# A pause in the due table of the weight conversions, in a fused attention and expert kernel

## The chip, the cores and the metric

One NeuronCore of a Trainium2 chip runs the whole kernel. The metric is the time of one execution on the device in microseconds (us). Five engines work beside one another, each on a queue of its own: PE (TensorE; its weight loads are shown as PEld), DVE (VectorE), ACT (ScalarE), POOL (GpSimd) and SP (SyncE), which here only issues DMAs.

## The reference

Causal attention in blocks of 64 over 8 batches of 8 heads (sequence 576, head size 64), then a feed-forward layer (512 to 2048 to 512) on its output:

```python
scores = scale * np.matmul(q, k.transpose(0, 1, 3, 2))
scores = np.where(mask, scores, -1000000000.0)
scores = scores - np.max(scores, axis=-1, keepdims=True)
attn = np.exp(scores)
attn = attn / (np.sum(attn, axis=-1, keepdims=True) + 1e-09)
attn_out = np.matmul(attn, v)
x = attn_out.transpose(0, 2, 1, 3).reshape(B * S, H * D)
h = x @ w_in
g = h * (1.0 / (1.0 + np.exp(-1.702 * h)))
return g @ w_out
```

The inputs q, k and v are float32. The two weight matrices are float64, and the kernel makes float32 of their bits itself, from the two 32-bit words of each weight.

## The kernel before, in words

**Attention by turns.** Two heads make a pair, and there are 32 pairs. Turn n (n from 0) computes the scores of pair n and the sums of values of pair n-1. A turn is a list of slots, written out by hand (ORDER, START for turn 4, HANDOVER for turn 8). In a slot stands a dash or one item:

- digits such as `1+0`, `2/3`, `4`: scores of these chunks of queries (`score`: matmuls into a PSUM bank, line 351 adds the mask and finds the maximum on DVE, line 358 is the exponential on ACT, lines 368 and 371 turn the sums into factors on DVE, line 376 scales on POOL, into the tile `turned` in the first 8 turns)
- `B`, `C`, `a`: flips of the weights of attention on PE (`flip`, line 102), moved out of PSUM by ACT (lines 411 and 424)
- `V`: the sums of values of pair n-1 (`av`, ACT lines 450 and 451 bring them to the tile `xr`), and the value loads of a later pair (`load_v`, lines 287 and 290)
- `L`: `prep` of pair n+1: two transposes on DVE (line 297, q first and then k), and then, into the buffer that they have just read, the eight loads of q and k of pair n+2 (`load`, line 279)

A slot's position is twice the turn plus its part of the turn. The list of turn 4, and the one of turns 5 to 7, are

```python
START = "1+0 - B 2/3 L C - V - 4 - a - - -"
"1+0 - B - 2 - C - 3 L V - a - 4 -",
```

so that L of turn 4 stands at position 8.67, its V at 9.07, its `4` at 9.33, and L of turn 5 at 11.25.

**The expert layer by tiles.** The 4608 tokens are 12 tiles of 384. For each of 16 slices of 128 columns of the hidden layer (`fc`), 12 matmuls sum into `hp`, ACT (line 562) and DVE (563) make `g` of it, ACT (571) its high part `gh` and POOL (82) the low part `gl`, and 9 matmuls sum `g` times the output weights into `acc`, one slice later. Matmuls take float32r, so that each operand is a high and a low part, and a product is three matmuls. Tile 0 starts after the sums of values of pair 3 (V of turn 4); from there on its matmuls stand between the items of the turns, as many after each slot as TILES_BY says. All matmuls are recorded at lines 99 and 102, helpers that keep PE in the order of the program.

**The weights by pieces.** 32 pieces of 128 by 512 weights, in groups of 8: four pieces of w_in, then four of w_out. Slices 4g to 4g+3 need group g: `hp` all four w_in pieces (8g to 8g+3, one after another), `acc` of slice fc the piece 8g + 4 + fc % 4. Each piece is two steps:

- `merge` (step 2j), on DVE: lines 223, 229 and 234 make float32 of the two words. Before it stands `begin` (line 219, ACT), which scales the high word into the PSUM bank `w3`, the only one for this
- `split_weights` (step 2j+1): the high part on ACT (line 243, tile `wih` or `woh`), the low part on POOL (line 82, `wil` or `wol`). With it go the load of piece j+2 on SP (line 202) and the `begin` of piece j+1

```python
if odd:
    split_weights(j)
    if j + 1 < len(pieces):
        load_weights(j + 3)
        begin(j + 1)
```

**What sets the order.** After each slot the loop at the end calls `convert` with the number of pieces due by then: WEIGHTS_BY, read off by linear interpolation at the slot's position less 0.5, and doubled and rounded down for steps (lines 631 and 632). So the table says where in the program a step, its loads and its begin are emitted. A slice of tile 0 also calls `convert` for what it needs (line 543), if it isn't emitted yet. The framework then gives each engine one fixed queue when the program is built. Matmuls keep the program's order; of the other instructions it takes the one earliest in the program among those that are ready by its own estimates of times. On the chip each engine works through its queue in that order.

Of the kernel before, what the change touches and what calls it, by code (L numbers as in the profile page):

```python
# [32 lines left out]
HANDOVER = "B C - 3+0/2+1 - - V - - - 4 - - L - -"  # L33


WEIGHTS_BY = ((0, 0), (8, 13), (14.5, 32))
TILES_BY = ((8.4, 0), (17, 1), (33.7, 4), (65.7, -2))


# [1 line left out]
def attention_moe_kernel(  # L41
# [204 lines left out]
    def convert(upto):  # L246

        while conv["step"] < int(2 * upto):
            j, odd = divmod(conv["step"], 2)
# [5 lines that stand above are left out]
            else:  # L255
                if j == 0:
                    begin(0)
                merge(j)
            conv["step"] += 1
# [322 lines left out]
    def quota(pos):  # L582
        xs, ys = zip(*TILES_BY)
        return -1.0 if pos < xs[0] else np.interp(pos, xs, [ends[y if y >= 0 else y - 1] for y in ys])
# [39 lines left out]
    for n in range(NPAIR + 1):  # L624
        items = step(n)
        for sl, fn in enumerate(items):
# [4 lines left out]
            pos = 2 * (n + (sl + 1) / len(items))  # L631
            convert(min(len(pieces), np.interp(pos - 0.5, *zip(*WEIGHTS_BY))))
            lim = quota(pos)
# [31 lines left out]
```

## Time and profile before

| | us |
|---|---|
| median of 3 runs | 1123.53 |
| lowest and highest | 1121.69 and 1123.55 |
| the profiled execution | 1120.49 |
| its span, first to last instruction | 1118.6 |
| busy: ACT | 498.6 (45%) |
| busy: POOL | 406.7 (36%) |

The rows that follow below are from this profiled execution. A row of a group has the line, the engine, what is written and read, shapes, the count, and the shortest, middle and longest duration in ns. A row of the timeline has the start in us, the duration in us, the engine ("SPq" is SP's issuing of DMAs), the line, the operation and the tiles; in brackets stand the idle time before it and what ended it. For a DMA the duration is that of its issue. Times count from the start of the span.

### The profile page before, as it was taken

The page shows a single profiled execution, that of the slowest core. Times are in us where ns is not written, and L with a number is a line of the kernel's source. Part 1 is how long each engine was busy: PE and PEld are TensorE (multiplying, and loading weights), DVE is VectorE, ACT ScalarE, POOL GpSimd, SP SyncE. Part 2 cuts the span into 40 slices and gives each one's busy share as a digit, 9 for nine tenths or more (in the row PEclk, how much of TensorE's full clock was granted, in tenths as well). Part 3 has the DMA queues.
Part 4 walks back from the last instruction along what each step waited for, and adds up shares of the span by engine and source line. Part 5 has one row for each costly group of instructions (what it writes and reads, how often), then busy time and mean ns, then how long its engine had stood idle before and what let it go on. Part 6 is the DMA issues. An engine that isn't in the chain of part 4 may idle for free. (4 is left out here: it accounts for less than half of the span.)

```text
span 1118.6 us, 19977 instructions
## 1 busy us (share of the span) xinstructions
PE 1076.4 (96%) x6960; PEld 908.7 (81%) x6960; DVE 583.0 (52%) x1856; ACT 498.6 (45%) x1321; POOL 406.7 (36%) x509
## 2 busy tenths in 40 slices
PE   5969998999999999999999999999999999999998
PEld 3757776788888888888888888888888888899997
DVE  6776885545545555654555655645545654211210
ACT  5866776434534433534443543444434444322322
POOL 4665664333333332333333333333333233122222
PEclk9979999999999999999999999999999999999999
DMA  8734532332444432343443333344342332200000
GB/s 171 205 89 153 150 73 62 84 79 57 105 86 86 103 80 64 64 98 78 98 101 74 75 93 65 70 108 85 81 107 63 71 85 58 54 29 1 29 1 29
DMA packets 219365, 91.25 MB, mean 82 GB/s; under 512 B 197760, under 2 KB 197760, under 8 KB 219264
## 3 DMA queue, kind: packets, MB, share of 16 engines
q1 hardware_dynamic: 214528, 89.38, 34.0%
q10 hardware_dynamic: 4736, 0.59, 0.3%
q8 instruction: 55, 0.90, 0.3%
q14 instruction: 46, 0.38, 0.1%
HBM read 45.09 MB, written 9.44 MB: 49 GB/s over the span
## 5 line engine op out<-in xcount | busy, mean ns | idle before, releaser
L82 POOL TENSOR_TENSOR gl<-g,gh 128x384 fp32r<-128x384 f32 x192 | 194.7, 1014 | 551.5 <-ACT gh L571 449.1
L99 PE MATMUL hp<-xh,wih 128*128 128x384 f32 x768 | 264.7, 345 | 7.9 <-DVE g L563 6.9
L563 DVE SCALAR_TENSOR_TENSOR g<-g,hp 128x384 f32<-128x384 f32 x192 | 105.9, 552 | 319.1 <-ACT g L562 317.8
L99 PE MATMUL hp<-xh,wil 128*128 128x384 f32 x768 | 258.4, 336 | 0.1
L562 ACT ACTIVATE g<-hp 128x384 f32<-128x384 f32 x192 | 94.1, 490 | 359.8 <-PE hp L99 354.8
L99 PE MATMUL hp<-xl,wih 128*128 128x384 f32 x768 | 253.9, 338 | 0.4 <-DVE xl L82 0.4
L99 PE MATMUL acc<-woh,gh 128*128 128x512 f32 x576 | 233.9, 406 | 0.0
L99 PE MATMUL acc<-wol,gh 128*128 128x512 f32 x576 | 226.9, 394 | 0.0
L99 PEld LDWEIGHTS hp<-xh,wih 128*128 128x128 f32 x768 | 144.2, 188 | 34.1 <-DVE g L563 23.1
L99 PE MATMUL acc<-woh,gl 128*128 128x512 f32 x576 | 167.9, 393 | 0.3 <-POOL gl L82 0.3
L571 ACT CAST gh<-g 128x384 fp32r<-128x384 f32 x192 | 98.4, 513 | 156.5 <-DVE g L563 156.4
L99 PEld LDWEIGHTS hp<-xh,wil 128*128 128x128 f32 x768 | 144.3, 188 | 6.5 <-POOL wil L82 0.7
L358 ACT ACTIVATE e<-e,mx 64x64 f32<-64x64 f32 (+4 forms) x240 | 132.3, 552 | 37.6 <-DVE mx L351 37.6
L376 POOL TENSOR_TENSOR e<-e,sm 64x64 f32<-64x64 f32 (+1 forms) x192 | 113.6, 612 | 95.0 <-DVE sm L371 46.5
L99 PEld LDWEIGHTS hp<-xl,wih 128*128 128x128 f32 x768 | 143.6, 188 | 1.3 <-DVE xl L82 1.3
L99 PE MATMUL bank<-qk 64*128 64x320 f32 (+4 forms) x768 | 122.5, 428 | 14.5 <-DVE qk L297 11.1
L99 PEld LDWEIGHTS acc<-woh,gh 128*128 128x128 f32 x576 | 107.9, 187 | 34.2 <-issue 10.5
L99 PEld LDWEIGHTS acc<-woh,gl 128*128 128x128 f32 x576 | 107.8, 188 | 25.9 <-POOL gl L82 1.2
L99 PEld LDWEIGHTS acc<-wol,gh 128*128 128x128 f32 x576 | 108.3, 188 | 16.7 <-POOL wol L82 0.3
L351 DVE CUSTOM_DVE_ANT_0 e<-bank,mask 64x64 f32<-64x64 f32 (+4 forms) x240 | 89.7, 417 | 56.9 <-PE bank L99 52.8
L385 DVE STREAM_TRANSPOSE turned<-e 128x384 f32<-128x384 f32 (+1 forms) x192 | 92.3, 499 | 48.8 <-POOL e L376 48.3
L99 PEld LDWEIGHTS bank<-qk 64*128 64x128 f32 x768 | 69.6, 193 | 54.2 <-issue 25.4
(50 smaller groups left out, 956.0 us busy)
## 6 DMA issues: line engine op xcount, KB each, us to landing
turned<-turned SPq DMA_DIRECT2D x192, 80.0 KB, 2.1
turned<-turned SPq DMA_DIRECT2D x96, 112.0 KB, 2.2
raw<-in_q_dram SPq DMA_DIRECT2D x128, 72.0 KB, 2.4
out_dram<-osb SPq DMA_DIRECT2D x36, 256.0 KB, 2.2
raw<-in_k_dram SPq DMA_DIRECT2D x120, 72.0 KB, 2.6
turned<-turned SPq DMA_DIRECT2D x96, 88.0 KB, 2.1
words<-in_moe_w_in_dram SPq DMA_DIRECT2D x16, 512.0 KB, 6.3
vp<-in_v_dram SPq DMA_DIRECT2D x60, 128.0 KB, 2.4
```

The lines of the kernel that those rows point to most:

```text
L82: eng.tensor_tensor(out=out, in0=in0, in1=in1, op=ALU.subtract)
L99: return tc.keep_in_program_order(nc.tensor.matmul(**kw))
L351: nc.vector.tensor_tensor_reduce(out=e[0:m, hd, lo:hi], in0=s, in1=mk, op0=ALU.add, op1=ALU.min, scale=-0.125, scalar=3e38 if lo == 0 else ...
L358: nc.scalar.activation(out=e[0:m, hd], in_=e[0:m, hd], func=AF.Exp, scale=-1.0, bias=mx[0:m, i, hd : hd + 1], accum_out=sm[0:m, i, hd : hd ...
L376: nc.gpsimd.tensor_tensor(out=x, in0=x, in1=sc.to_broadcast([m, width(i)]), op=ALU.mult)
L385: nc.vector.transpose(out=tw[:, :, SLOT[i] : SLOT[i] + i, hd].rearrange("p b j c -> p j b c"), in_=e[:, hd, 0 : i * P],)
L562: nc.scalar.activation(out=g, in_=hp[:, 0:tt], func=AF.Tanh, scale=1.702)
L563: nc.vector.scalar_tensor_tensor(out=g, in0=g, scalar=1.0, in1=hp[:, 0:tt], op0=ALU.add, op1=ALU.mult)
L571: nc.scalar.copy(out=gh, in_=g)
```

## The change

One constant is changed, the table of due pieces:

```diff
-WEIGHTS_BY = ((0, 0), (8, 13), (14.5, 32))
+WEIGHTS_BY = ((0, 0), (7.5, 12), (8.8, 12.5), (14.5, 32))
```

Between the points 7.5 and 8.8 (slot positions 8.0 to 9.3, turn 4 up to its `4`) the table grows by half a piece only. Before it the slope is 1.6 pieces for a unit of position and was 1.625; after it 3.42, and was 2.92. In steps (half pieces) due after a slot:

| position | slot | steps before | steps after |
|---|---|---|---|
| 5.43 | dash before V, turn 2 | 16 | 15 |
| 6.71 | dash before L, turn 3 | 20 | 19 |
| 8.00 | end of turn 3 | 24 | 24 |
| 8.53 | `2/3`, turn 4 | 26 | 24 |
| 9.20 | dash after V, turn 4 | 30 | 24 |
| 9.47 | dash after `4`, turn 4 | 31 | 26 |
| 11.00 | dash before `3`, turn 5 | 40 | 36 |
| 11.25 | L, turn 5 | 42 | 38 |
| 11.50 | dash after V, turn 5 | 43 | 40 |
| 13.00 | dash before `3`, turn 6 | 52 | 50 |
| 13.25 | L, turn 6 | 53 | 52 |
| 14.13 | `1+0`, turn 7 | 58 | 58 |
| 15.00 | dash after C, turn 7 | 64 | 64 |

Step 2j+1 counts as done at 2j+2; with it the load of piece j+2 is emitted. No instruction is added or taken away.

## The prediction

> **What bounds the kernel now.** I read the page's busy times first, then PE by stretches of 10 us over the time in which weights are converted, then what PE waited for in it.
>
> ```profile
> PE 1076.4 (96%) x6960; PEld 908.7 (81%) x6960; DVE 583.0 (52%) x1856; ACT 498.6 (45%) x1321; POOL 406.7 (36%) x509
> 60.00:70.00 10.00, 6.08 (x19) 3.57 (x18) 7.82 (x26) 7.67 (x24) 5.05 (x7) 0.52 0.87 215
> 70.00:80.00 10.00, 9.08 (x83) 7.57 (x82) 8.07 (x16) 6.24 (x18) 6.54 (x8) 0.80 0.07 29
> 120.00:130.00 10.00, 8.23 (x49) 6.35 (x50) 9.52 (x32) 8.02 (x23) 6.45 (x6) 1.00 0.55 166
> 130.00:140.00 10.00, 10.00 (x54) 7.72 (x53) 7.43 (x19) 6.82 (x18) 7.05 (x11) 1.00 0.44 123
> 180.00:190.00 10.00, 6.91 (x43) 5.69 (x43) 3.16 (x10) 5.58 (x16) 5.09 (x5) 1.00 0.06 13
> 900.00:1000.00 100.00, 99.75 (x639) 87.33 (x638) 36.38 (x110) 35.69 (x87) 28.21 (x33) 1.00 0.22 57
> ```
>
> In a stretch's row the columns after the length are busy PE, PEld, DVE, ACT and POOL, the granted clock, the DMA share and GB/s. PE is the bound over the whole span, and late in it (900 to 1000) it hardly pauses, so what PE loses before 200 us is carried to the end, and what it wins there too. The question is only what the change does to PE's pauses up to 200 us. From 82 us on, when the first expert slice is through, these are:
>
> ```profile
> PE bank L102 <- ACT turned L411: 3.5, 3, 1.6
> PE bank L102 <- POOL turned L376: 3.1, 2, 2.0
> PE bank L99 <- DVE mx L351: 2.5, 4, 1.5
> PE hp L99 <- DVE g L563: 1.8, 1, 1.8
> ```
>
> (Total, number, longest.) That is 10.9 us between 82 and 205 us, none of it put down to a converted weight. The weights come just in time, though, as the rows of the third part show.
>
> **What the change moves.** It removes and adds no instruction. Up to the start of turn 4 the due table falls by at most one step in a slot; from there to the end of turn 6 it is 1 to 6 steps (half pieces) lower. Two things follow.
>
> First the conversions' own order. A piece is a chain over three engines with one PSUM buffer:
>
> ```profile
> L219 ACT ACTIVATE wm<-words x28: 612/633/662, 13.2 to 159.3; 128x512 f32<-128x512 f32 x28
> L223 DVE TENSOR_SCALAR wm<-wm x32: 658/699/700, 18.1 to 180.3; 128x512 uint32<-128x512 uint32 x32
> L243 ACT CAST woh<-wm x16: 617/620/641, 57.9 to 183.9; 128x512 fp32r<-128x512 f32 x16
> L82 POOL TENSOR_TENSOR wol<-wm,woh x16: 1262/1286/1302, 60.3 to 185.9; 128x512 fp32r<-128x512 f32 x16
> ```
>
> The 28 first halves (line 219) are pieces 0 to 27 in order, the last at 159.28, so any of them can be counted. The table asks for all 64 steps by the middle of turn 7, yet the last low part starts at 185.9, among the scalings of that turn's last score, nearly half a turn later: the chain runs several pieces behind its due table, at the pace of its own links. A due time that moves while the chain is behind it changes nothing by itself. I cost this part at nothing; its cover is that backlog.
>
> Second, the loads. The split of piece j also issues the load of piece j+2, on SP, and SP's issues stand in the trace in the order in which the program emits them. Behind the loads of q and k for a later pair (line 279) an issue is stuck until the transposes of line 297 free the buffer:
>
> ```profile
> 88.59 0.77 DVE L297 STREAM_TRANSPOSE qk<-raw 128x576 f32<-128x576 f32 x1
> 89.39 1.95 SPq L279 DMA_DIRECT2D raw<-in_q_dram  x4
> 91.39 2.12 SPq L279 DMA_DIRECT2D raw<-in_k_dram  x4
> 93.55 0.50 SPq L202 DMA_DIRECT2D words<-in_moe_w_out_dram  x1
> 98.18 0.64 ACT L219 ACTIVATE wm<-words 128x512 f32<-128x512 f32 x1
> 101.17 0.63 ACT L243 CAST woh<-wm 128x512 fp32r<-128x512 f32 x1
> 110.49 0.77 DVE L297 STREAM_TRANSPOSE qk<-raw 128x576 f32<-128x576 f32 x1
> 111.64 0.63 ACT L219 ACTIVATE wm<-words 128x512 f32<-128x512 f32 x1
> ```
>
> The load at 93.55 is piece 15's, the first behind the eight q/k loads of pair 6. Piece 14 begins at 98.18 and is split at 101.17; then the chain stands still until 111.64, where piece 15 begins, 0.38 us after the transpose that uses those q/k loads has ended. Its load had been issued 18 us before. So the fixed order of ACT, made when the program is built, counts a load behind the q/k loads as landing only with them. I take this from the place of the row; it is what the forecast hangs on.
>
> By the due tables four sets of loads change sides. Piece 11 goes behind the q/k loads of pair 5 (split 9 is due after the slot L of turn 3, not before it), piece 14 behind those of pair 6 (split 12 at 9.47, past L of turn 4 at 8.67), pieces 20 and 21 behind those of pair 7 (splits 18 and 19 at 11.25 and 11.50, L at 11.25), piece 27 behind those of pair 8. (Piece 9 passes the four value loads of pair 3; the backlog hides that.) The issues themselves are SP's and nothing waits for SP's time.
>
> **The cost.**
>
> ```profile
> 84.94 0.65 ACT L219 ACTIVATE wm<-words 128x512 f32<-128x512 f32 x1
> 90.99 0.62 ACT L219 ACTIVATE wm<-words 128x512 f32<-128x512 f32 x1
> 131.69 1.27 POOL L82 TENSOR_TENSOR wil<-wm,wih 128x512 fp32r<-128x512 f32 x1
> 133.95 0.34 PE L99 MATMUL hp<-xh,wil 128*128 128x384 f32 x1
> 135.06 1.28 POOL L82 TENSOR_TENSOR wol<-wm,woh 128x512 fp32r<-128x512 f32 x1 [2.10 <-ACT woh L243]
> 135.27 0.65 ACT L219 ACTIVATE wm<-words 128x512 f32<-128x512 f32 x1
> 139.43 0.63 ACT L219 ACTIVATE wm<-words 128x512 f32<-128x512 f32 x1
> 154.40 0.64 ACT L219 ACTIVATE wm<-words 128x512 f32<-128x512 f32 x1
> 159.28 0.64 ACT L219 ACTIVATE wm<-words 128x512 f32<-128x512 f32 x1
> 161.29 1.28 POOL L82 TENSOR_TENSOR wil<-wm,wih 128x512 fp32r<-128x512 f32 x1
> 162.62 0.44 PE L99 MATMUL hp<-xh,wil 128*128 128x384 f32 x1
> 163.11 1.28 POOL L82 TENSOR_TENSOR wil<-wm,wih 128x512 fp32r<-128x512 f32 x1 [0.54 <-ACT wih L243]
> 164.44 0.44 PE L99 MATMUL hp<-xh,wil 128*128 128x384 f32 x1
> ```
>
> Step 1. Piece 11 begins where piece 12 did (90.99 for 84.94), pieces 12 and 13 in the places of 13 and 14, and then the pause comes one piece earlier: piece 14 begins at 111.64. Pieces 14 to 19 stand in the places of 15 to 20. Before, piece 19's low part ends at 131.69 + 1.27 = 132.96 and PE reads it at 133.95, a slack of 0.99. In piece 20's place it ends at 135.06 + 1.28 = 136.34: PE waits 136.34 - 133.95 = 2.4 us in hp of slice 8. Queued behind on PE are the rest of that slice and the scores and flips of turn 6, and for these DVE and ACT wait.
>
> Step 2. Piece 20 now has a load behind the q/k loads of pair 7. It begins between 135.27 (piece 21's place, if the load holds nothing) and 139.43 (the place of piece 22, the first behind these loads before). Neither row says which, since piece 22's predecessor ended just then: I take the middle, 137.35.
>
> Step 3. From piece 15 to 27 the pace is (159.28 - 111.64) / 12 = 3.97 us. Six pieces on, piece 26 begins at 161.2 (159.1 to 163.3) in place of 154.40: 6.8 us late (4.7 to 8.9). It has no slack: its low part ends at 161.29 + 1.28 = 162.57 and PE reads it at 162.62; for piece 27 it is 164.39 and 164.44. So by hp of slice 12 PE is 6.7 us late, 4.3 of them new.
>
> Step 4, what comes back. At the end of turn 7 PE waits for POOL's scaling, with the last piece's low part between the two:
>
> ```profile
> 185.97 0.33 PE L102 MATMUL bank<-ident,turned 128*128 128x128 f32 x1 [1.07 <-POOL turned L376]
> 188.30 1.20 PE L102 MATMUL bank<-ident,turned 128*128 128x128 f32 x9 [2.00 <-POOL turned L376]
> 100.58 0.63 PE L102 MATMUL bank<-ident,turned 128*64 128x128 f32 x4 [1.42 <-ACT turned L411]
> 129.40 0.63 PE L102 MATMUL bank<-ident,turned 128*64 128x128 f32 x4 [1.60 <-ACT turned L411]
> ```
>
> The last pieces come one pace (4.0 us) later while PE comes 6.7 later, so they stand 2.7 us further ahead of it, and of the 3.07 us of these two waits I let 2.7 go (bounds 0 and 3.07). Sum: 2.4 + 4.3 - 2.7 = +4.0 us, with ends at 4.7 - 3.1 = +1.6 and +8.9.
>
> The profiled execution took 1120.49 us, its span 1118.6; the sum makes 1124.5 of it. The median of the runs shown is 1123.53, 3.04 above it, so the forecast in these terms is **1127.5**, its own range 1125.1 to 1132.4.
>
> [...] The granted clock was 0.52 from 60 to 70 us and 0.80 from 70 to 80, in a stretch where PE was busy for 6.08 of 10 us; from 180 to 190, with PE busy for 6.91, it stayed 1.00. [...] It makes the last rival.
>
> **The rivals.**
>
> Nothing moves (1123.5). For it: the chain is behind its table, the loads are really issued long before their use (93.55 against 111.64), so the change wouldn't do what it says. If only the place of the loads in ACT's order held it up and that stays, all slots stay. Against it: 0.99 us is all the cover that piece 19 has. Within 2 us of 1123.5.
>
> Faster (1120.5). With piece 14 out of the stretch from 98 to 101, 0.64 + 0.63 us of ACT stand no longer ahead of the evictions (line 411) for which PE waits at 100.58, and the like a turn later at 129.40: 1.42 + 1.60 = 3.0 us less. It needs the chain to catch up in the pause up to 111, and decides at one point: whether piece 19's low part is there when PE reads it, that is, whether the chain is late by less than 0.99 us at 133.95. Against it: in my reading another piece stands in that place.
>
> The clock falls (1134.3). If the waits at 134 or 163 bring what happened at 60: lost there 10 x (0.48 + 0.20) = 6.8 us on top of the +4.0.
>
> **How the numbers follow.** Forecast 0.47, nothing moves 0.24, faster 0.22, clock 0.07. A measurement of this kernel tells about 0.2% (2.2 us) from no change. Of the forecast 0.03 falls within that bound, of the rival without motion 0.02 above it: faster 0.22, same 0.26, slower 0.52. The range from 1119.5 to 1132.5 holds the forecast, the case of no motion and over half of the faster one, and leaves the clock out.
>
> **What would show it.** Right: the pause of line 219 stands between its 14th and 15th row (before: 15th and 16th), PE has waits "hp <- POOL wil" of some us near 134 and 163, the two waits for POOL near 188 shrink. Wrong: a chain without the pause from 101 to 111, or piece 19's low part before 134; then the load order isn't what holds ACT, and the sum falls to the rivals. A second pause before piece 20 tells step 2's ends apart.

## The result, and the profile after

| | before | after |
|---|---|---|
| median (us), runs beside one another | 1123.94 (6 runs) | 1130.31 (6 runs) |
| lowest and highest | 1121.69, 1124.98 | 1129.31, 1131.00 |
| the profiled execution, its span | 1120.49, 1118.6 | 1130.80, 1128.9 |

The changed kernel is slower: the ratio is 1.0063 with a 95% interval of 1.0053 to 1.0073, and the medians differ by 6.4 us (1.0057). Executions of one kernel differ in the mean clock that they were granted: of the 71 of the kernel before that stand beside the experiments, 6 had 0.992 (1120.2 to 1120.8 us) and 17 had 0.986 (1124.5 to 1126.2); the profile of before had 0.992, that of the changed kernel 0.984. The forecast of 1127.5 had the sign, and the range to 1132.5 holds the time; the median is 2.8 us above the forecast.

The page of the changed kernel, busy times and one group of its costliest (busy time and mean ns; then the idle time before the group, and what ended it):

```profile
PE 1084.2 (96%) x6960; PEld 915.3 (81%) x6960; DVE 582.0 (52%) x1856; ACT 498.0 (44%) x1321; POOL 406.7 (36%) x509
L99 PE MATMUL hp<-xh,wil 128*128 128x384 f32 x768 | 259.5, 338 | 2.7 <-POOL wil L82 2.7
```

The counts are those of before, so nothing was added. New is that PE idles 2.7 us for the low parts of converted weights. PE's busy time is 7.8 us longer for the same 6960 matmuls: part of them ran slower, and the clock below says where.

The forecast's first sign is the place of the pause in ACT's queue. ACT's timeline of the changed kernel, with the transpose of DVE that stands beside it:

```profile
99.05 0.64 ACT L219 ACTIVATE wm<-words 128x512 f32<-128x512 f32 x1
102.51 0.62 ACT L243 CAST woh<-wm 128x512 fp32r<-128x512 f32 x1
112.12 0.77 DVE L297 STREAM_TRANSPOSE qk<-raw 128x576 f32<-128x576 f32 x1
113.28 0.63 ACT L219 ACTIVATE wm<-words 128x512 f32<-128x512 f32 x1
```

The row at 99.05 begins piece 13, the 14th of line 219, and the next begin waits until 113.28. It starts 0.39 us after the end of the transpose (112.12 + 0.77 = 112.89), as the 16th did before (0.38 us). The pause stands one piece earlier, and the piece after it is 14. The load itself is not late: it had landed at 99.75, 13.5 us before this begin, and ACT idles for 2.63 us ahead of 112.24. It is the place in ACT's queue that holds the begin.

PE's timeline of the changed kernel at slices 8 and 12, and at the end of turn 7:

```profile
134.96 0.34 PE L99 MATMUL hp<-xh,wil 128*128 128x384 f32 x1
136.58 0.45 PE L99 MATMUL hp<-xh,wih 128*128 128x384 f32 x1 [1.11 <-ACT wih L243]
137.93 0.69 PE L99 MATMUL hp<-xh,wil 128*128 128x384 f32 x1 [0.91 <-POOL wil L82]
138.74 0.63 PE L99 MATMUL acc<-woh,gh 128*128 128x512 f32 x1
...
168.80 0.44 PE L99 MATMUL hp<-xh,wih 128*128 128x384 f32 x1 [0.78 <-ACT wih L243]
170.15 0.44 PE L99 MATMUL hp<-xh,wil 128*128 128x384 f32 x1 [0.91 <-POOL wil L82]
...
173.03 0.44 PE L99 MATMUL hp<-xh,wih 128*128 128x384 f32 x1 [1.17 <-ACT wih L243]
174.38 0.45 PE L99 MATMUL hp<-xh,wil 128*128 128x384 f32 x1 [0.91 <-POOL wil L82]
...
195.17 0.63 PE L102 MATMUL bank<-ident,turned 128*64 128x128 f32 x4 [1.35 <-ACT turned L411]
...
198.77 1.20 PE L102 MATMUL bank<-ident,turned 128*128 128x128 f32 x9 [1.48 <-POOL turned L376]
```

In slice 8 PE waits for the high part of piece 19 and then for its low part; in slice 12 for both parts of pieces 26 and 27. Before, there was no such wait. (A wait costs PE up to 0.2 us more than its bracket says: matmuls that don't wait overlap, as the one at 134.96 lasts 0.34 us and the next starts at 135.13.) From the last low part at 137.93 on, the matmuls take longer: 0.69 us for hp with wil, which behind a wait of the same length took 0.45 at 174.38, and 0.63 for the first of acc, which took 0.40 at 174.84. That is the clock, which is 0.50 for the 3.41 us from 137.73 on. The same kernel by stretches (busy PE, PEld, DVE, ACT, POOL, then granted clock, DMA share, GB/s):

```profile
130.00:140.00 10.00, 7.05 (x29) 5.14 (x30) 7.13 (x17) 5.79 (x15) 7.17 (x10) 0.89 0.46 135
140.00:150.00 10.00, 10.00 (x96) 8.36 (x94) 6.13 (x15) 6.05 (x14) 4.05 (x4) 0.94 0.43 93
170.00:180.00 10.00, 7.76 (x30) 4.95 (x31) 5.31 (x14) 4.74 (x11) 5.05 (x6) 0.83 0.25 76
190.00:200.00 10.00, 7.17 (x43) 5.75 (x44) 3.94 (x14) 5.13 (x13) 4.46 (x4) 1.00 0.00 0
```

The clock was 1.00 in all four of these stretches before. From 130 to 150 it now lacks 1.1 + 0.6 = 1.7 us of full speed, from 170 to 180 the same: each is a stretch of 3.41 us at half rate, from 137.73 and from 175.28.

**Where the time went.** PE keeps the order of the program, so the start of the same matmul can be compared from trace to trace. Starts of hp of some slices (matmuls numbered by tile and slice; slice 16 is the first of the next tile), from the traces, in us; the last two columns belong to runs that are told of below:

| hp of slice | before | after | changed kernel again | old loads |
|---|---|---|---|---|
| 3 | 92.83 | 95.78 | 92.94 | 95.66 |
| 4 | 100.96 | 102.57 | 99.73 | 103.79 |
| 8 | 131.24 | 132.78 | 129.94 | 134.09 |
| 9 | 137.49 | 143.05 | 140.12 | 140.34 |
| 12 | 160.99 | 166.57 | 163.63 | 163.86 |
| 13 | 168.13 | 179.65 | 176.70 | 170.98 |
| 16 | 201.88 | 212.37 | 209.41 | 206.32 |
| end | 1118.62 | 1128.92 | 1126.94 | 1123.01 |

Between the two profiles: +2.95 up to slice 3, which the last two columns will show to be no work of the change; -1.41 from 3 to 8; +4.02 in slice 8; nothing from 9 to 12; +5.94 in slice 12; -1.03 from 13 to 16; little after that. The gain ahead of slice 4 is a wait that went. Before, PE waited 1.42 us for ACT's evictions at 100.58; in the changed kernel PE's timeline shows the same flips without a pause (14 in one row, where before 10 ended before the wait and 4 came after it):

```profile
100.86 1.95 PE L102 MATMUL bank<-ident,turned 128*128 128x128 f32 x14
102.57 0.42 PE L99 MATMUL hp<-xh,wih 128*128 128x384 f32 x1
```

In slice 8 the last low part is read at 137.93 in place of 133.95, 3.98 later, of which 1.54 was there at the slice's start: 2.44 are the waits, and the other 1.6 stand behind them, at half clock. In slice 12 it is 174.38 for 164.44, 9.94 later, less 5.58: 4.36 are the waits, and 1.6 the clock. In all: 6.8 us of waits and 3.2 us of clock, less 1.4 us before slice 8 and 1.0 us at the tail, or 7.6 us from slice 3 to slice 16 (10.49 - 2.95 = 7.54 by the table).

### The profile page after: what moved, and what is told of

It reads as the page before. It is cut to its first block, busy times and chain, and to the rows that moved or that the text cites. A ratio compares the mean times of both kernels' runs of the same rounds, so it can differ in the third digit from the quotient of the medians.

```text
span 1128.9 us, 19982 instructions
## 1 busy us (share of the span) xinstructions
PE 1084.2 (96%) x6960; PEld 915.3 (81%) x6960; DVE 582.0 (52%) x1856; ACT 498.0 (44%) x1321; POOL 406.7 (36%) x509
```

## The experiments

The theory to be tested (A): the due table as such is worth nothing, because the chain of conversions runs behind it; the time hangs on which weight loads (line 202) stand on SP's side ahead of the q/k loads of a pair (line 279) and which behind, since the queues put the begin of the first piece behind them after that pair's transposes. SP's issues in the traces show the places: 12, 15, 22 and 28 weight loads stand ahead of the q/k loads of pairs 5 to 8 before, and 11, 14, 20 and 27 in the changed kernel. Its rivals: the due dates themselves do it (other instructions are ordered otherwise), or it is the clock alone.

All ratios are to the kernel before on the same chip, with 95% intervals. The medians of before were 1123.26 (27 runs, 1120.37 to 1126.16) beside the first four, 1122.93 (15) beside the next four, and 1122.90 (29) beside the three late ones.

| kernel | median us | ratio |
|---|---|---|
| new table, old loads | 1123.18 (11) | 0.9999 [0.9990, 1.0008] |
| only piece 14's load moved | 1125.42 (11) | 1.0016 [1.0006, 1.0026] |
| new table, loads to 14 as of old | 1129.09 (5) | 1.0051 [1.0038, 1.0063] |
| new table, loads from 19 as of old | 1125.92 (11) | 1.0026 [1.0017, 1.0036] |
| only loads 20 and 21 moved | 1127.82 (5) | 1.0042 [1.0029, 1.0054] |
| old table, one load ahead | 1122.20 (11) | 0.9995 [0.9986, 1.0004] |
| old table, three ahead | 1128.60 (5) | 1.0055 [1.0042, 1.0067] |
| new table, three ahead | 1129.86 (5) | 1.0058 [1.0045, 1.0070] |
| one ahead from piece 14 on | 1118.87 (12) | 0.9970 [0.9959, 0.9981] |
| three ahead from piece 14 on | 1119.49 (12) | 0.9970 [0.9959, 0.9981] |
| five ahead from piece 14 on | 1124.81 (12) | 1.0019 [1.0009, 1.0029] |

### The new table with the loads of the old one

The edits of the experiments are shown in short; this one is against the kernel before:

```diff
-WEIGHTS_BY = ((0, 0), (8, 13), (14.5, 32))
+WEIGHTS_BY = ((0, 0), (7.5, 12), (8.8, 12.5), (14.5, 32))
+LOADS_BY = ((0, 0), (8, 13), (14.5, 32))
...
+            load_weights(min(28, int(np.interp(pos - 0.5, *zip(*LOADS_BY))) + 2))
             convert(min(len(pieces), np.interp(pos - 0.5, *zip(*WEIGHTS_BY))))
```

> The new due table for the conversions, with the loads of pieces up to 27 emitted at the places of the old table. Theory A (the place of the loads among the q/k loads on SP is all that matters): 1124, within 2 us of before; PE waits for POOL wil in hp of slices 8 and 12 below 0.3 us in all. Theory B (it matters when the steps themselves are due, few in turn 4 and more after it): as the changed kernel, 1130, with 2 us of waits at slice 8 and about 4 at slice 12.

Measured: 1123.18, a ratio of 0.9999. In the two traces the instructions of all engines, SP's issues among them, stand in the same order, one for one. So the due dates of the conversions alone order nothing, and the whole loss belongs to the places of the loads. The rival that the due dates do it falls here.

Since its order is that of before, this kernel shows something else: what one and the same order gives in another execution. Its span is 1123.0, 4.4 us more than that of before. Three stretches of it, and PE's two waits at the end of turn 7:

```profile
20.00:30.00 10.00, 8.33 (x55) 5.53 (x55) 9.77 (x34) 8.37 (x23) 8.03 (x11) 0.84 0.84 214
80.00:90.00 10.00, 8.20 (x33) 6.44 (x31) 6.18 (x13) 4.01 (x8) 4.33 (x4) 0.83 0.00 0
190.00:200.00 10.00, 8.30 (x49) 6.38 (x51) 3.89 (x16) 5.27 (x15) 1.85 (x5) 0.83 0.00 1
```

```profile
188.87 0.33 PE L102 MATMUL bank<-ident,turned 128*128 128x128 f32 x1 [1.08 <-POOL turned L376]
191.20 1.44 PE L102 MATMUL bank<-ident,turned 128*128 128x128 f32 x9 [2.00 <-POOL turned L376]
```

The waits are before's (1.07 and 2.00), but here the clock falls behind the second one, to 0.83 from 190 to 200, where before's profile has 1.00; and likewise from 20 to 30 and from 80 to 90 (0.84 and 0.83, before 1.00 in both). The way from hp of slice 13 to slice 16 takes 35.34 us here and 33.75 in before's profile. A part of what separates two profiles is thus the granted clock (a mean of 0.986 here, 0.992 in before's) and no work of any change, and before's profile (1120.49, near the fastest of its runs) was a lucky one.

### Single loads moved

Only piece 14's load goes behind the q/k loads of pair 6; the table is the old one:

```diff
-                    load_weights(j + 3)
+                    load_weights(j + 3 if j != 12 else 0)
```

> The old due table, with one load moved: that of piece 14 goes behind the q/k loads of pair 6. Theory A: the pause of line 219 stands one piece earlier (before piece 14, from about 101 to 111 us), all later pieces are one pace (4 us) late, PE waits 2.4 us in hp of slice 8 and some 2 more at slice 12: 1128 (1126 to 1130). Theory B: as before, 1124, since the table is the old one.

Measured: 1125.42, slower by 0.16%, some 2 us where 4 to 5 were expected: the pause stands before piece 14 and the wait at slice 8 is there, the size was not right. PE's timeline at slice 8 in this kernel:

```profile
135.59 0.45 PE L99 MATMUL hp<-xh,wil 128*128 128x384 f32 x1 [0.91 <-POOL wil L82]
```

At slice 12 PE waits only 0.23 us for a low part. The chain has not caught up there: pieces 22 to 26 begin 3.7 to 4.2 us later than before (piece 26 at 158.45 for 154.40). PE has fallen behind by nearly as much. From hp of slice 8 (131.65 for 131.24) to hp of slice 12 (164.68 for 160.99) it loses 3.3 us: 1.3 in slice 8, and 2.0 between slices 9 and 12, most of it in waits for other work (1.03 for a maximum of DVE, 0.25 and 0.89 for evictions of ACT, where before had one of 0.46). Why these came stays open. Some of the loss is offset ahead of slice 8 (1.0 us from slice 3 on). The clock is 1.00 from 130 to 180 and 0.83 from 190 to 200, behind the waits at the end of turn 7, as in the kernel with old loads.

The counterpart, the new table with the loads up to piece 14 at their old places and the later ones as in the change (this line and the next two stand where the line with 28 stands above):

```diff
+            load_weights(min(15, int(np.interp(pos - 0.5, *zip(*LOADS_BY))) + 2))
```

> The new due table, with the loads of pieces up to 14 at the places of the old table, those from 15 on as in the changed kernel (20, 21 and 27 behind the q/k loads). Theory A: pieces 14 to 19 are in time and slice 8 has no wait; the chain pauses before piece 20, which begins near 137 to 139 us in place of 131; PE waits 3 to 6 us in hp of slice 12; clock at 1.00 from 130 to 160 us; 1128 (1126 to 1130). Theory B: as the changed kernel, 1130, waits at slice 8 too.

Measured: 1129.09, slower by 0.51%. There is no wait at slice 8. The loss comes at slice 12, which takes 7.6 us longer than before's; the clock is 0.88 from 160 to 170 and 0.61 from 170 to 180, which is 10.2 us at half rate.

And the other way round: 11 and 14 as in the change, from position 10 on the old places:

```diff
+            load_weights(min(28 if pos > 10 else 0, int(np.interp(pos - 0.5, *zip(*LOADS_BY))) + 2))
```

> The new due table, with the loads of pieces 11 and 14 as in the changed kernel (behind the q/k loads of pairs 5 and 6), those emitted from turn 5 on at the places of the old table. Theory A: PE waits 2.4 us in hp of slice 8 and the granted clock falls there for some 3 us (1.6 us lost), no second pause before piece 20, little wait (under 2 us) at slice 12: 1128 (1126 to 1129.5). Theory B: as the changed kernel, 1130, with 4 us of waits at slice 12.

Measured: 1125.92, slower by 0.26%, just below the expected range; the fall of the clock expected at slice 8 did not come (1.00 from 130 to 140). PE's timeline in it has the wait of slice 8, and next to nothing for weights at slice 12 (the gain of 1.3 us ahead of slice 4 is there too, and in none of the kernels with 11 and 14 at their old places):

```profile
135.65 0.44 PE L99 MATMUL hp<-xh,wil 128*128 128x384 f32 x1 [0.91 <-POOL wil L82]
...
168.10 0.45 PE L99 MATMUL hp<-xh,wil 128*128 128x384 f32 x1 [0.24 <-POOL wil L82]
```

The clock is 1.00 from 130 to 150 and from 160 to 180 in this kernel, and between 150 and 160 no matmul of hp lasts over 0.44 us; within that time PE loses 3.6 us from hp of slice 8 to hp of slice 12 (131.42 to 164.75, before 131.24 to 160.99), with the same three waits of 1.03, 0.25 and 0.89 us as when only piece 14's load is moved. So the clock alone is not the cause. Over the whole span its mean is 0.988 in this kernel, 0.986 in the one with old loads and 0.992 in before's profile.

Last of these, only pieces 20 and 21 go behind the q/k loads of pair 7:

```diff
+            load_weights(min(20 if pos < 11.6 else 28, int(np.interp(pos - 0.5, *zip(*LOADS_BY))) + 2))
```

> The new due table; of all loads up to piece 27 only those of pieces 20 and 21 stand behind the q/k loads of pair 7, the others (27 too) at the places of the old table. Theory A1 (the pause before piece 20 makes most of the cost): no wait at slice 8, piece 20 begins near 138 to 139 us on before's scale, PE waits some 3 to 4.5 us in hp of slice 12; 1127.5 (1126 to 1129). Theory A2 (piece 27 behind the q/k loads of pair 8 makes most of it): 1124, little wait at slice 12.

Measured: 1127.82, slower by 0.42%. PE's timeline at slice 12, and the clock there:

```profile
162.72 0.44 PE L99 MATMUL hp<-xh,wil 128*128 128x384 f32 x1 [0.62 <-POOL wil L82]
165.35 0.44 PE L99 MATMUL hp<-xh,wil 128*128 128x384 f32 x1 [1.83 <-POOL wil L82]
168.89 0.69 PE L99 MATMUL hp<-xh,wih 128*128 128x384 f32 x1 [0.92 <-ACT wih L243]
170.23 0.69 PE L99 MATMUL hp<-xh,wil 128*128 128x384 f32 x1 [0.66 <-POOL wil L82]
```

```profile
160.00:170.00 10.00, 6.21 (x27) 3.84 (x25) 6.77 (x14) 5.08 (x13) 7.78 (x11) 0.80 0.09 16
170.00:180.00 10.00, 9.77 (x67) 7.01 (x69) 5.97 (x17) 3.73 (x10) 3.65 (x5) 0.69 0.38 101
```

The clock lacks 2.0 + 3.1 = 5.1 us here, which is 10.2 us at half rate. Slice 12 takes 8.4 us longer than before's: 4.0 us are waits by the brackets, and most of the rest is the clock's.

In total the two parts come near the whole: piece 14 alone costs 1125.42 - 1123.26 = 2.2, pieces 20 and 21 alone 1127.82 - 1122.93 = 4.9, together 7.1, where the change costs 6.4. That is partly luck, since the parts are made up otherwise: the change has 3.4 us of half rate at slice 12 and not 10.2, and nothing of the 2.0 us between slices 9 and 12. Pieces 11 and 27 were not moved alone; the kernels with them (1.0026 and 1.0051) differ from those without (1.0016 and 1.0042) by 0.1%, within the intervals.

### More loads ahead

If a load on the wrong side costs, one on the right side could gain. One load ahead for all pieces, with the old table:

```diff
-                    load_weights(j + 3)
+                    load_weights(max(j + 3, min(j + 4, 28)))
```

> The old due table, every load up to piece 27 emitted one split earlier (split j loads piece j+3). Theory A: each pause falls one piece later (before 13, 16, 23), the chain is one pace (4 us) earlier after it, no wait for weights at slices 8 and 12, and of the two waits for POOL near 188 us (3.1 us) a part goes: 1122 (1120 to 1124). If the chain being earlier is worth nothing, 1123.3.

Measured: 1122.20, no difference (0.9995, interval over 1). The expected time came, but not by the expected road; PE's timeline shows a loss and a gain:

```profile
61.83 1.33 PE L99 MATMUL bank<-qk 64*128 64x192 f32 x8 [5.19 <-DVE qk L297]
...
185.48 0.63 PE L102 MATMUL bank<-ident,turned 128*64 128x128 f32 x4 [0.49 <-ACT turned L411]
...
188.29 1.20 PE L102 MATMUL bank<-ident,turned 128*128 128x128 f32 x9 [0.68 <-POOL turned L376]
```

At the tail the waits are 1.17 us in place of 3.07. But at 61.83 PE waits 5.19 us for the transposes of pair 4, where it waited 2.52 before:

```profile
58.69 0.76 PE L99 MATMUL bank<-qk 64*128 64x192 f32 x8 [2.52 <-DVE qk L297]
```

One more weight load stands ahead of that pair's q/k loads (6 for 5). Those loads themselves are not late: the last of them had landed at 38.2 before and lands at 38.7 here, some 20 us before the second transpose (57.88 before, 61.00 here). It is DVE's fixed order that sets the transposes later, as ACT's does with the begins: one more merge (58.87 to 61.09, after 0.91 us of waiting for its begin) now stands between the two transposes. With three ahead (`j + 6` for `j + 4`):

> The old due table, every load up to piece 27 emitted three splits earlier (split j loads piece j+5). Theory A: pauses before pieces 15, 18 and 25, the chain two to three paces earlier at slices 8 and 12 and done before the scaling of turn 7's last score, so the two waits for POOL near 188 us (3.1 us) go: 1121 (1119 to 1123). Against it: more conversions within turns 3 to 5, where DVE is busy for 9 to 10 us of 10 near 55 us, so that the waits of PE for DVE, ACT and POOL there grow by more than 3 us: 1124 to 1128.

Measured: 1128.60, slower by 0.55%: the expectation failed, and the direction that it named as speaking against it came. PE's timeline of this kernel:

```profile
68.45 1.33 PE L99 MATMUL bank<-qk 64*128 64x192 f32 x8 [11.26 <-DVE qk L297]
```

The wait has grown by (11.26 - 2.52) / 3 = 2.9 us for each load, after 5.19 - 2.52 = 2.7 for one. Late in it the kernel gains: it is 8.15 us behind the one with old loads at hp of slice 8, and 2.46 at slice 16. The same loads with the new table (its line 36 beside this edit):

> The new due table, every load up to piece 27 emitted three splits earlier (split j loads piece j+5). Theory A: none of the slow waits at slices 8 and 12, the same order of work as the old table with these loads wherever the chain is behind its table: within 2 us of that kernel, 1121 (1119 to 1124). Theory B (the steep table after turn 4 itself costs): 1128 or more, with waits at slice 12.

Measured: 1129.86, slower by 0.58%, with the same wait (11.25 us). The expected 1121 was missed for the same reason; that the two tables differ little once the loads are ahead (1.3 us, intervals that overlap) is what theory A says.

What is left is to move loads ahead only where no early pair pays. Loads up to piece 13 stay; from 14 on one ahead:

```diff
-                    load_weights(j + 3)
+                    load_weights(max(j + 3, min(j + 4, 28) if j > 10 else 0))
```

> As the one with three ahead from piece 14 on, but only one ahead. Theory: the 2.7 us that one load ahead of the fourth pair's q/k loads cost are not paid, and the gain of about 3.2 us at the tail stays, less what the other kernels show as their run to run spread: about 1121, between 1119.5 and 1123. Rival: a wait of 2 to 3 us at a later transpose of L297 takes the gain: 1123 to 1124.

Measured: 1118.87, **faster** than before by 0.30% and below the expected 1119.5 to 1123, and three ahead (`j + 6`):

> The old due table; the loads of the weight pieces up to 13 stay at their old places, and each later load is issued with the split three pieces earlier than before. Theory: the loss of the kernel with all loads three ahead came from loads put ahead of the fourth pair's q/k loads (11.26 us of waiting at 68.45); those stay where they were, so the wait before the fourth turn is that of before (2.5 us at about 58.7), there is no wait for wih or wil at slices 8 and 12, and the tail's waits for POOL (1.07 and 2.00 us) go: about 1120, between 1118.5 and 1122. Rival: the wait only moves to the transposes of the sixth or seventh pair, because more loads stand ahead of their q/k loads: 1126 or more, with a wait for a transpose of L297 after 90 us of the span. Second rival: the tail isn't worth its waits, and nothing is gained: 1123.3.

Measured: 1119.49, a ratio of 0.997 as well. PE's timeline of the kernel with one ahead from piece 14 on:

```profile
58.77 1.33 PE L99 MATMUL bank<-qk 64*128 64x192 f32 x8 [2.52 <-DVE qk L297]
...
184.26 0.63 PE L102 MATMUL bank<-ident,turned 128*64 128x128 f32 x4 [0.49 <-ACT turned L411]
...
187.06 1.20 PE L102 MATMUL bank<-ident,turned 128*128 128x128 f32 x9 [0.68 <-POOL turned L376]
```

The wait before turn 4 is before's 2.52, there is none for wih or wil, and the tail has 1.17 us of waits in place of 3.07, with the clock at 1.00 behind them (190 to 200). The lowest times are 2.7 us apart (1117.53 and 1120.19), less than the medians (4.0), so part of the gain may be the clock's at the tail. With five ahead (`j + 8`):

> Five ahead from piece 14 on. Theory: the tail holds no wait for POOL with three ahead already, so two more bring nothing: within 1 us of the kernel with three ahead. Rival: more loads ahead of the q/k loads of the sixth to eighth pair delay their transposes, and it is slower than with three ahead by 2.7 us for each load more, up to 5 us.

Measured: 1124.81, slower than before by 0.19% and than three ahead by 5.3 us. The rival's price came, but not by its road. ACT's timeline of this kernel, then PE's:

```profile
146.94 0.62 ACT L243 CAST wih<-wm 128x512 fp32r<-128x512 f32 x1 [1.75 <-DVE wm L234]
147.46 0.63 ACT L219 ACTIVATE wm<-words 128x512 f32<-128x512 f32 x1
150.38 0.62 ACT L243 CAST wih<-wm 128x512 fp32r<-128x512 f32 x1 [2.29 <-DVE wm L234]
150.90 0.62 ACT L219 ACTIVATE wm<-words 128x512 f32<-128x512 f32 x1
151.46 0.58 ACT L451 COPY xr<-bank 128x512 f32<-128x512 f32 x1
```

```profile
142.94 2.98 PE L99 MATMUL bank<-turned,vp 128*64 128x128 f32 x60
152.09 1.06 PE L102 MATMUL bank<-ident,turned 128*64 128x128 f32 x4 [4.37 <-ACT xr L451]
```

The sums of values were through on PE at 145.92. ACT's queue now holds two casts and their begins ahead of the copy that PE needs (line 451), and each cast waits for DVE first (1.75 and 2.29 us). PE stands 4.37 us for these casts, the second of which (through at 151.00) it reads at 170.28 only, and the clock is 0.66 from 150 to 160, which is 6.8 us at half rate. Too early costs here as too late did.

### The changed kernel once more

> The changed kernel itself, profiled once more. The waits for the converted weights come from fixed queues and should stand again: about 2 us in hp of slice 8, about 4 us in hp of slice 12. Open is the granted clock. If the two stretches of 3.41 us at half clock (137.7 and 175.3) follow from the waits alone, both come back at their places and the piece of work from hp 8 to hp 12 is as long as in the first profile to within 0.3 us. [...]

Measured: one time of 1128.82, with one of 1122.90 for the kernel before. PE's waits in this second profile, and the clock around them:

```profile
133.74 0.45 PE L99 MATMUL hp<-xh,wih 128*128 128x384 f32 x1 [1.11 <-ACT wih L243]
135.09 0.69 PE L99 MATMUL hp<-xh,wil 128*128 128x384 f32 x1 [0.91 <-POOL wil L82]
165.85 0.44 PE L99 MATMUL hp<-xh,wih 128*128 128x384 f32 x1 [0.77 <-ACT wih L243]
167.19 0.45 PE L99 MATMUL hp<-xh,wil 128*128 128x384 f32 x1 [0.91 <-POOL wil L82]
170.09 0.44 PE L99 MATMUL hp<-xh,wih 128*128 128x384 f32 x1 [1.17 <-ACT wih L243]
171.44 0.45 PE L99 MATMUL hp<-xh,wil 128*128 128x384 f32 x1 [0.91 <-POOL wil L82]
```

```profile
130.00:140.00 10.00, 7.98 (x36) 6.09 (x35) 6.99 (x14) 4.68 (x13) 5.02 (x6) 0.83 0.55 113
170.00:180.00 10.00, 9.00 (x66) 6.28 (x68) 6.10 (x17) 4.40 (x12) 4.40 (x4) 0.83 0.40 101
```

The waits agree with the first profile to 0.01 us, and both half-clock stretches come back behind them. By the table of starts, slices 8 and 12 take 10.18 and 13.07 us here, 10.27 and 13.08 in the first profile, and 6.25 and 7.14 before. So both the waits and the clock's falls behind them are what the change costs; the gain from slice 3 to 8 (1.41 us) and that of the tail come again as well. What differs is the time up to slice 3, which starts 2.84 us earlier than in the first profile of the same program and 0.11 us later than before: the +2.95 there is no work of the change.

## Why the prediction was right, and where it was short

**The place of the pause** was right: it stands between the 14th and 15th begin, and the new table with the old loads (0.9999) shows that the loads, not the due dates, put it there.

**Step 1** said 2.4 us in slice 8; the waits cost 2.44. **Steps 2 and 3** said 4.3 more by slice 12; they cost 4.36. Piece 26 begins at 164.45 for 154.40; less the 1.54 us that PE stood late at slice 8 and the 1.6 us of clock it is 6.9 us late, where 6.8 was forecast. Of step 2's ends neither is right as a picture: piece 20 begins at 136.99, which less the 1.54 us is 135.45, near the early end, but its cast comes only at 142.64, 5.65 us after its begin, where piece 21 in that place took 3.64 before (135.27 to 138.91). The middle price came out right by this other way, and that was luck; why the cast came so late stays open.

**Step 4**, the return, was mis-sized: 2.7 us were to come back, and 1.0 did. The two waits near 188 had been 3.07 us; in the changed kernel two waits of 1.35 and 1.48 stand at the same items, the first now for an eviction of ACT. The kernel with old loads takes 1.6 us longer over that stretch than before's profile, with the clock at 0.83; measured against that the return is 2.6.

**The clock** was a rival with a chance of 0.07 and a price of 6.8 us on top. It came, at half the price: 3.2 us, two stretches of 3.41 us at 0.50. The forecast's sum had nothing for it, and this is the term that made it short. A second term that it lacked, the wait of 1.42 us at 100.58, went the other way. By the profiles the change costs 2.44 + 4.36 + 3.2 - 1.4 - 1.0 = 7.6 us, and 6.0 if the tail is set against the kernel with old loads; by the medians it costs 6.4, between the two. Behind these two tail waits the clock stays at 1.00 in before's profile and is 0.83 from 190 to 200 in two others (old loads, piece 14's load moved); so the return of 2.6 is likely the usual one, but the share over all runs is not known.

The argument on the clock was drawn from two waits, 1.07 and 2.00 us (185.97 and 188.30), behind which the clock of before stayed at 1.00. That it stays full behind waits of this size was not shown beyond that one profile, and it misled. In the kernel with old loads the clock fell behind those same two waits (0.83 from 190 to 200), and in the changed kernel during the second of two waits of 1.11 and 0.91 us with matmuls between them (0.50 from 137.73 to 141.14); in its second profile the same two waits came with 0.83 from 130 to 140.

**The rivals.** "Nothing moves" fell with the changed pause and the waits. "Faster" was to decide at piece 19's low part, late by less than 0.99 us or by more; it came 3.4 us late (137.88, less the 1.54 us, for 132.96), 2.4 more than its slack. Half of its gain came all the same: the wait at 100.58 went, though not for the reason given, since a cast and a begin (98.54 and 99.05) still stand ahead of the evictions there. What moved the evictions was not isolated. The second wait, 1.60 us at 129.40, stands at 130.93 in the changed kernel with 1.59.

## What to carry to other kernels

Where a build-time order works off a table of due dates, look first at what is emitted along with the work: here the loads, and which other loads on the same issuing queue they stand ahead of or behind, were worth all of 0.6%, and the dates nothing. A load's place is a trade: here 2.7 to 2.9 us of a later transpose in DVE's order for each load put ahead of pair 4's (ahead of pair 6's and 7's one or three more cost no such wait), against the waits for late weights; the best version moves only those loads for which no one pays (1118.87 for 1122.90), and going further loses it again. When waits of a microsecond or two are added in front of matmuls, budget the clock that may fall with them as well: here it was 3.2 us beside 6.8.

## What was not expected of the hardware

- Two waits of 1.11 and 0.91 us came with half rate in both profiles of the changed kernel: 0.50 for the 3.41 us from 137.73 on in the first, and 0.83 from 130 to 140 in the second, which is as long. It began before the second wait had ended (137.73 for 137.93); in the second profile the matmul behind that wait (135.09) already lasts 0.69 us, where one behind a wait of the same length lasts 0.45 at 167.19. Behind one wait of 0.91 us (only piece 14's load moved, or loads from 19 as of old) the clock stayed at 1.00 from 130 to 140.
- Whether it falls can differ for the same order and the same waits: behind 1.07 and 2.00 us not in one profile (1.00 from 190 to 200), in another it did (0.83). With it go some 1.6 us, and the stretches at 0.84, 0.83 and 0.83 (20 to 30, 80 to 90, 190 to 200) lie where the 4.4 us between two spans of the same order arise: +2.83 at slice 3, nothing more up to slice 13, +1.59 from there to slice 16.
- What decides it is not shown. In the changed kernel's profile PE was busy for 1.60 of the 3.42 us ahead of 137.73, for 1.34 of the 3.41 us ahead of 175.28 and for 1.83 of the 3.41 us ahead of 28.50, and the clock was 0.50 for 3.41 us from each of the three on. In before's profile PE was busy for 1.80 of the 3.41 us from 186.69 to 190.10, and the clock stayed at 1.00.
